# Attention, mixture of experts and feed-forward on one core: stores issued late, ten strided units first, single PSUM banks at attention's end, zero matmuls that read data, extra run fifth

## The chip, the cores and the metric

The kernel runs on one NeuronCore of a Trainium2 chip. It is one program with five instruction queues: TensorE (PE, its weight loads shown as PEld), VectorE (DVE), ScalarE (ACT), GpSimd (POOL) and the queue that only starts transfers (SP). Transfers between memory and SBUF are shared by 16 DMA engines. The metric is the device time of the whole program in microseconds (us). One execution with the hardware profiler gives the trace from which all rows come.

## The reference

Causal attention in 4 batches of 576 positions with 8 heads of 64: heads 0 to 3 attend to the last 32 positions ("local"), heads 4 to 7 to earlier positions of the same residue modulo 32 ("strided"). The result, 2304 tokens of 512 features, goes through a mixture of 8 experts of which each token takes one, then through a feed-forward layer with a squared ReLU.

```python
scores = where(mask, q @ k.T / 8, -1e9); x = softmax(scores) @ v      # mask: local or strided
logits = x @ w_gate + modality_bias[modality_id]
e = argmax(logits, 1); gate = softmax(logits)[e]
x[e == i] = gate * (relu(x[e == i] @ w1[i]) @ w2[i])                  # for each expert i
out = relu(x @ w_in) ** 2 @ w_out
```

All is float32. The products of the experts and of the feed-forward layer are made of three products each, on operands split in a rounded part ("hi") and its rest ("lo").

## The kernel before

**Attention.** The work is cut in 40 units: 22 strided ones of up to 108 tokens and 18 local ones of 128 tokens (`units`). A step k of the loop over units issues, for several units at once, the stages of a pipeline: `norm(k-4)` (VectorE divides by the sum of the softmax, into the tile `xn`, and POOL stores `xn` in the table `x1` in memory), the loads of a later group of units (`loads_to`, on SP), `stage_s(k)` (scores, PE), maximum and subtraction (VectorE) and the exponential (ScalarE), `features(k-5)` (transposed copy of `xn` into `xT`, products with the gate's weights), `stage_t(k-2)` (PE transposes the probabilities) and `stage_v(k-3)` (product with v). Seven strided units come first, then strided and local ones in turn, and three local ones last. Loads go in groups of one or two units into `NLD` buffers. Each engine runs its own instructions in the order in which they are written and waits on semaphores for the others; `stage_s` issues `KEEP` matmuls of zeros (`warm`).

**The end of attention** (from `stage_t(L - 1)` on) finishes the last five units with PSUM tiles of two banks ("sp", "xp") and three times six matmuls of zeros (`dense`). Then the gate's logits of the last tiles are made: `products` (gate's weights times `xT`), `fetch` (ScalarE copies them), `folds` (PE sums them), `add` (VectorE adds the bias), `rt.local` (VectorE: maximum, one-hot `oh`).

**Routing** (`Routing.finish`) counts the tokens of each expert (`cp`), finds every token's place in the sorted order (`pos`, `pab`), builds one-hot matrices `ohb` (by VectorE, ScalarE and POOL, 18 slices) and `pay`, and multiplies them in 18 matmuls into `ip`, the sorted list of tokens (`idn`). `keep(n)` issues n matmuls of zeros, 512 columns each.

**Experts** (`moe_and_ffn`). The sorted list is worked off in nine runs of 256 places and one extra run of 128 (for places in which a second expert begins), each of 8 chunks. A chunk loads 512 KB of an expert's weights (SP), splits them (ScalarE hi, VectorE lo), and PE does `mm1` and `mm2`. In between, by a table of chunks (`conv`), 16 halves of the feed-forward layer's weights (512 KB each, `load_half`) are loaded and converted. POOL gathers the tokens of a run by an indirect transfer. A loop (`extra_loop`) for further extra runs is in the program and is not entered with these inputs. **The feed-forward layer** follows, 6 blocks of 384 tokens.

Of the kernel before, what the change touches and what calls it, by code (L numbers as in the profile page):

```python
# [33 lines left out]
N2A = 7  # L34
NCV = 4
HOLD = 5
KEEP_R = (6, 11, 24)
KEEP_D = 6
# [4 lines left out]
S_FIRST = 7  # L43
NWM = 5
NLD = 8
# [28 lines left out]
def attention_and_routing(es, tc, a, x1, res):  # L74
# [8 lines left out]
    ps = es.enter_context(tc.tile_pool(name="a_ps", bufs=2, space=PSUM))  # L83

    def bank(tag):
        if tag == "xp":
            return ps.tile([128, 2, 512], F32, tag=tag, name=tag, bufs=1)[:, 0]
        return ps.tile([128, 512], F32, tag=tag, name=tag, bufs=1)
# [12 lines left out]
    rt.spare = lambda: ps.tile([128, 2, 512], F32, tag="sp", name="dm")  # L101
# [4 lines left out]
    while ns < NST or nl < NTL - 3:  # L106
        if nl < NTL - 3 and (ns == NST or nl * (NST - S_FIRST) <= (ns - S_FIRST) * (NTL - 3)):
# [8 lines left out]
    for kind, sizes in (("s", (1, 1, 1) + (2,) * 9 + (1,)), ("l", (1, 1) + (2,) * 8)):  # L116
        t0 = 0
        for n in sizes:
            groups.append((kind, t0, n))
            t0 += n  # L120
# [147 lines left out]
    def v_norm3(k):  # L268
        kind, t, n, w, gi, o = geom(k)
        xn = wk.tile([128, 256], F32, tag="xn", name="xn", bufs=8)  # L270
# [3 lines left out]
        )  # L274
        if kind == "l":
# [10 lines left out]
        st[k, "x"] = xn  # L286

    def stage_x(k, xq):
# [5 lines left out]
        if kind == "l":  # L294
            ac.activation(out=xT[:, 0:2, 128 * t:128 * t + 128], in_=src, func=AF.Copy)
            return
# [13 lines left out]
        while c < end:  # L310
# [5 lines left out]
            ac.activation(out=tok, in_=src[:, :, a0:a0 + NJ * m].rearrange("p c (m j) -> p c m j", j=NJ), func=AF.Copy)  # L316
# [19 lines left out]
    def fetch(t0, t1, src):  # L336
        lt = wk.tile([128, 256], F32, tag="lt", name="lt", bufs=2)[:, 0:128 * (t1 - t0)]
        ac.activation(out=lt, in_=src[:, 0:128 * (t1 - t0)], func=AF.Copy)
        return t0, t1, lt
# [61 lines left out]
    for k in range(NU):  # L401
        if k >= LN:
            norm(k - LN)
        side(1)
# [26 lines left out]
    def two(tag):  # L431
        return ps.tile([128, 2, 512], F32, tag=tag, name=tag + "t", bufs=1 if tag == "xp" else 2)
# [5 lines left out]
    stage_t(L - 1)  # L438
    norm(L - 3)
    stage_x(L - 4, bank("xq"))  # L440
    sb = two("sp")
    stage_v(L - 2, sb[:, 0])
    sc = two("sp")
    stage_t(L, sc[:, 0])
    if lt_p:
        add(folds(lt_p.pop(0), sc[:, 1]))
    xb = two("xp")
    stage_v(L - 1, xb[:, 0])
    stage_x(L - 3, sb[:, 1])
    stage_v(L, xb[:, 1])  # L450
    norm(L - 2)
    norm(L - 1)
    t0, t1 = lg_done[0], lg_ready(L - 2)
    assert t1 - t0 <= 2 and NTL - t1 == 3
    if t1 > t0:
        lq = bank("xq")
        products(t0, t1, lq)
        lt_p.append(fetch(t0, t1, lq))
    lp = bank("pp")
    products(t1, NTL - 1, lp, (2, 3))  # L460
    norm(L)
    sd = two("sp")
    dense(sd[:, 1], KEEP_D)
    stage_x(L - 2, sd[:, 0])
    if lt_p:
        add(folds(lt_p.pop(0), bank("xq")))
    todo += [rt.local(loc, t1)]
    se = two("sp")
    dense(se[:, 1], KEEP_D)
    stage_x(L - 1, se[:, 0])  # L470
    products(t1, NTL - 1, lp, (0, 1))
    sf = two("sp")
    dense(sf[:, 1], KEEP_D)
    stage_x(L, two("xp")[:, 0])
    lt_p.append(fetch(t1, NTL - 1, lp))
    add(folds(lt_p.pop(0), bank("xq")))
    side(100)
    lr = sf[:, 0]
    products(NTL - 1, NTL, lr)
    add(folds(fetch(NTL - 1, NTL, lr), bank("pp")))  # L480
# [5 lines left out]
class Routing:  # L486
# [95 lines left out]
    def finish(self):  # L582
# [5 lines left out]
        def keep(n):  # L588
            for i in range(n):
                pe.matmul(dm[:, i % 2], lhsT=self.warm[:, 0:128], rhs=self.warm, start=True, stop=True)  # L590

        keep(KEEP_R[0])
        cp = bank("xp")
# [50 lines left out]
        for i in range(n_ac):  # L644
            ac.activation(out=ohb[:, nb + i, :], in_=self.iob, func=AF.Square, scale=-1.0, bias=pab[:, 1, nb + i:nb + i + 1])
        if n_ac:
            ac.activation(out=ohb[:, nb:nb + n_ac], in_=ohb[:, nb:nb + n_ac].bitcast(F32), func=AF.Relu, scale=-1.0, bias=1.0)
# [12 lines left out]
        order = list(range(nb, T)) + list(range(nb))  # L660
# [17 lines left out]
    def extras(self, buf, gs, idf):  # L678
# [6 lines left out]
        def t_(n):  # L685
# [5 lines left out]
                         in1=xv[:, 2, :].unsqueeze(2).to_broadcast(s7t), op=ALU.is_equal)  # L691
        pk = t_(7 * T).rearrange("p (x t) -> p x t", x=7)
        xs = t_(21).rearrange("p (q x) -> p q x", q=3)
        for qi, src in enumerate((idf, es_, gs)):
            ve.tensor_tensor(out=pk, in0=so, in1=src.unsqueeze(1).to_broadcast(s7t), op=ALU.mult)  # L695
            ve.tensor_reduce(out=xs[:, qi], in_=pk, axis=AX.X, op=ALU.add)  # L696
        ve.tensor_copy(res["xidn"], xs[:, 0])
        xm = t_(7)
        ve.tensor_tensor(out=xm, in0=xs[:, 1], in1=xv[:, 1, :], op=ALU.is_equal)
        ve.tensor_tensor(out=xs[:, 2], in0=xs[:, 2], in1=xv[:, 0, :], op=ALU.mult)  # L700
        ve.tensor_tensor(out=res["xgm"], in0=xm, in1=xs[:, 2], op=ALU.mult)

    def side_ops(self, op):
# [37 lines left out]
        def xruns():  # L741
            ve.tensor_tensor(out=w77, in0=self.lt7, in1=flb, op=ALU.mult)
            ve.tensor_reduce(out=rk, in_=w77, axis=AX.X, op=ALU.add)
            ve.tensor_tensor(out=sel, in0=self.k9[:, 0:7].unsqueeze(2).to_broadcast(s77),
                             in1=rk.unsqueeze(1).to_broadcast(s77), op=ALU.is_equal)
            ve.tensor_tensor(out=sel, in0=sel, in1=flb, op=ALU.mult)
            o7 = off[:, 1:8]
            ve.tensor_tensor(out=tmp1, in0=o7.unsqueeze(1).to_broadcast(s77), in1=o7.unsqueeze(2).to_broadcast(s77),
                             op=ALU.is_lt)
            ve.tensor_reduce(out=bx[:, 0], in_=tmp1, axis=AX.X, op=ALU.add)  # L750
            ve.tensor_single_scalar(out=bx[:, 1], in_=offf[:, 1, 1:8], scalar=128.0, op=ALU.is_le)
            ve.tensor_tensor(out=bx[:, 0], in0=bx[:, 0], in1=self.e17, op=ALU.subtract)
# [557 lines left out]
```

## Time and profile before

| | us |
|---|---|
| median of 3 runs (lowest, highest) | 771.91 (768.98, 772.53) |
| the profiled execution's own time | 772.12 |
| its span, first to last instruction | 770.3 |
| PE busy (share of the span) | 749.7 (97%) |
| VectorE, ScalarE, POOL busy | 422.1, 345.9, 92.6 |

The profiled execution lies 0.2 us above the median, and its own time 1.8 us above its span: the span is what the rows divide. "Busy" of PE counts matmuls whose ends are modelled, so a stretch of 100% isn't one at full speed. A row of a timeline gives the start and the length in us, and in brackets the engine's idle time ahead of it with what ended it. PEclk is the granted clock of TensorE as a share of 2.4 GHz (0.50 is 1.2 GHz).

### The profile page before, as it was taken

To read this page: it belongs to the slowest core of one execution; us is meant where nothing else is said; L and a number is where in the kernel's file an instruction comes from. 1 tells how busy PE (TensorE), PEld (TensorE's weight loads), DVE (VectorE), ACT (ScalarE), POOL (GpSimd) and SP (SyncE) were. 2 spreads that over 40 slices of the span, in tenths; PEclk is the share of its full clock that TensorE was granted. 3 is DMA by queue.
4 is the path that set the end of the run, shared out by engine and by line. 5 is a ranking of instruction groups with operands and counts; after the bars stand their busy time and mean duration, and the time that the engine had idled before them with its cause. 6 is when DMAs were issued, how large, how long until landed. Compare 5 with 4: busy or idle time off the path is not lost.

```text
span 770.3 us, 14540 instructions
## 1 busy us (share of the span) xinstructions
PE 749.7 (97%) x5785; PEld 672.5 (87%) x5787; DVE 422.1 (55%) x845; ACT 345.9 (45%) x678; POOL 92.6 (12%) x118
## 2 busy tenths in 40 slices
PE   9899979999999999999999999999999999999996
PEld 5676746999899999999898998989899899989995
DVE  5776856788878788874896322332332232233221
ACT  3554634566766666654776322322332232233221
POOL 8543422101100010000000100010010001001001
PEclk9999998999999999999999999999999999999999
DMA  8999206678776877763361100000010000001001
GB/s 216 277 275 262 81 24 224 197 256 264 249 255 222 272 236 233 236 206 123 119 185 53 41 1 1 14 27 1 1 43 0 1 14 28 0 1 42 1 0 42
DMA packets 31709, 90.97 MB, mean 118 GB/s; under 512 B 8050, under 2 KB 9282, under 8 KB 31638
## 3 DMA queue, kind: packets, MB, share of 16 engines
q1 hardware_dynamic: 23446, 75.27, 31.5%
q0 software_dynamic: 8192, 14.74, 5.8%
q8 instruction: 46, 0.75, 0.4%
q14 instruction: 25, 0.20, 0.1%
HBM read 80.52 MB, written 9.44 MB: 117 GB/s over the span
## 4 chain that ended last, share of the span: by engine, by line
PE 78%; DVE 2%; DMA 1%; ACT 1%; issue 1%; POOLq 0%; DVEq 0%
PE fhp L1040 26%; PE op L1065 26%; PE hp L829 13%; PE yp L840 13%; DVE w L799 1%; PE tp L818 1%; DMA stg<-in_wcat_dram 1%; ACT w L795 0%; DMA out_dram<-ob,idn 0%; DVE xl L822 0%; POOLq L1306 0%; DVE hl L834 0%; ACT xh L821 0%; DVE xt L695 0%; DVE xt L696 0%
## 5 line engine op out<-in xcount | busy, mean ns | idle before, releaser
L1040 PE MATMUL fhp<-xh,w 128*128 128x384 f32 x768 | 211.1, 337 | 0.0
L1052 DVE TENSOR_TENSOR r<-fhp,r 128x384 f32<-128x384 f32 x80 | 44.6, 558 | 223.0 <-ACT gh L1050 211.9
L1043 ACT ACTIVATE r<-fhp 128x384 f32<-128x384 f32 x96 | 47.1, 491 | 244.2 <-PE fhp L1040 244.2
L1040 PEld LDWEIGHTS fhp<-xh,w 128*128 128x128 f32 x768 | 140.6, 188 | 4.0
L1065 PE MATMUL op<-w,gh 128*128 128x512 f32 x546 | 141.9, 395 | 0.0
L1040 PE MATMUL fhp<-xl,w 128*128 128x384 f32 x384 | 130.1, 339 | 0.0
L1065 PEld LDWEIGHTS op<-w,gh 128*128 128x128 f32 x546 | 101.3, 188 | 16.9
L799 DVE TENSOR_TENSOR w<-stg,w 128x1024 fp32r<-128x1024 f32 x80 | 97.6, 1220 | 20.6 <-ACT w L795 19.4
L829 PE MATMUL hp<-xh,w 128*128 128x256 f32 (+1 forms) x640 | 101.4, 281 | 2.7 <-ACT w L795 1.5
L829 PEld LDWEIGHTS hp<-xh,w 128*128 128x128 f32 x640 | 87.3, 189 | 4.6 <-ACT w L795 1.9
L795 ACT ACTIVATE w<-stg 128x1024 fp32r<-128x1024 f32 x80 | 84.1, 1053 | 12.0 <-DVE mk L738 6.1
L840 PE MATMUL yp<-hh,w 128*128 128x256 f32 x576 | 81.0, 283 | 0.0
L1065 PE MATMUL op<-w,gl 128*128 128x512 f32 x273 | 78.2, 394 | 0.0
L1040 PEld LDWEIGHTS fhp<-xl,w 128*128 128x128 f32 x384 | 72.1, 188 | 3.9
L840 PEld LDWEIGHTS yp<-hh,w 128*128 128x128 f32 x576 | 73.3, 189 | 0.0
L1075 POOL DMA_INDIRECT out_dram<-ob,idn x18 | 18.8, 1043 | 441.7 <-ACT ob L1073 412.0
L1055 DVE TENSOR_TENSOR gl<-r,gh 128x384 fp32r<-128x384 f32 x91 | 50.8, 558 | 21.9 <-ACT r L1054 14.4
L832 ACT ACTIVATE hh<-hp 128x256 fp32r<-128x256 f32 (+1 forms) x80 | 29.8, 372 | 72.0 <-PE hp L829 70.9
L1065 PEld LDWEIGHTS op<-w,gl 128*128 128x128 f32 x273 | 51.4, 188 | 12.1
L829 PE MATMUL hp<-xl,w 128*128 128x256 f32 (+1 forms) x320 | 50.9, 281 | 0.0
L1050 ACT ACTIVATE gh<-r 128x384 fp32r<-128x384 f32 x91 | 47.8, 526 | 2.9
L840 PE MATMUL yp<-hl,w 128*128 128x256 f32 x288 | 45.8, 280 | 0.0
(219 smaller groups left out, 842.6 us busy)
## 6 DMA issues: line engine op xcount, KB each, us to landing
stg<-in_wcat_dram SPq DMA_DIRECT2D x80, 512.0 KB
stg<-in_w2cat_dram SPq DMA_DIRECT2D x32, 512.0 KB
qk<-in_qkl_dram SPq DMA_DIRECT2D x8, 576.0 KB
qk<-in_qks_dram SPq DMA_DIRECT2D x9, 432.0 KB
v<-in_vl_dram SPq DMA_DIRECT2D x8, 396.0 KB
x<-xn POOLq DMA_DIRECT2D x18, 128.0 KB, 6.9
x<-xn POOLq DMA_DIRECT2D x40, 54.0 KB, 7.8
v<-in_vs_dram SPq DMA_DIRECT2D x18, 111.4 KB
```

The costliest lines, as they stand in the source:

```text
L795: ac.activation(out=w[:, 0, :], in_=t, func=AF.Copy)
L799: ve.tensor_tensor(out=w[:, 1, :], in0=t, in1=w[:, 0, :].bitcast(F32), op=ALU.subtract)
L829: pe.matmul(hp, lhsT=w[:, wi, 128 * k:128 * k + 128], rhs=x[:, k, 0:n], start=(i == 0), stop=(i == 11))
L832: ac.activation(out=hh, in_=hp, func=AF.Relu)
L840: pe.matmul(yp[c // 2][:, SLOT * (c % 2):SLOT * (c % 2) + SLOT], lhsT=w[:, wi, 512 + 128 * c:640 + 128 * c], rhs=x, start=(j == 0 and x is ...
L1040: pe.matmul(hp, lhsT=w[:, wi, 128 * k:128 * k + 128], rhs=x[k], start=(i == 0), stop=(i == 11))
L1043: ac.activation(out=r, in_=hp, func=AF.Relu)
L1050: ac.activation(out=gh, in_=r, func=AF.Square)
L1052: ve.tensor_tensor(out=r, in0=hp, in1=r, op=ALU.mult)
L1055: ve.tensor_tensor(out=gl, in0=r, in1=gh.bitcast(F32), op=ALU.subtract)
L1065: pe.matmul(op[t], lhsT=x[:, 128 * t:128 * t + 128], rhs=w[:, wi, 512:1024], start=(j == 0 and first), stop=(j == NC2 - 1 and last))
L1075: gp.indirect_dma_start(out=out[:, :], out_offset=bass.IndirectOffsetOnAxis(ap=idn[:, i:i + 1], axis=0), in_=ob, in_offset=None,)
```

## The change

- A unit's store in `x1` is no longer written in `norm`, but taken from a list (`stores`) at the start of a later step, up to 16 units behind; `xn` has 20 buffers (8 before), loads have 7 (8 before).
- Ten strided units first (7 before), seven local ones last (3 before).
- At the end of attention a new pool of eight single banks takes the place of the two-bank tiles; the order of the stages is new, 2 matmuls of zeros stand where 18 stood, and the last tile's logits are made without the copy and the sum.
- In routing, six matmuls of zero weights read `oha` and `pay` as soon as these are written; `ohb` of ScalarE comes in two pieces, and the 18 matmuls take another order. `keep` has 7, 9 and 12 matmuls (6, 11 and 24).
- At the start of the experts the first loads and splits have a new order, nine matmuls read the first split weights (`busy`), and both gathered blocks are scaled by ScalarE.
- The extra run is the fifth of ten (third before). Its small VectorE work (29 instructions) goes out two at a time, one pair a chunk. The 16 halves are spread over 62 chunk positions which leave out ten around the extra run.

```diff
-KEEP_R = (6, 11, 24)          -KEEP_D = 6     -S_FIRST = 7      -NLD = 8
+KEEP_R = (7, 9, 12)           +KEEP_D = 2     +S_FIRST = 10     +NLD = 7
+XR = 4                        +DEFER = 16     +L_LAST = 7
...
     def v_norm3(k):
-        xn = wk.tile([128, 256], F32, tag="xn", name="xn", bufs=8)
+        xn = wk.tile([128, 256], F32, tag="xn", name="xn", bufs=DEFER + 4)
...
+        stores.append((k, xn))
...
+    def store():
+        k, xn = stores.pop(0)
         kind, t = geom(k)[0:2]
         if kind == "l":
             gp.dma_start(out=x1[t * 128:t * 128 + 128, 0:256], in_=xn)
...
         if k >= LN:
             norm(k - LN)
+        while len(stores) > max(1, min(DEFER, DEFER + 20 - k)):
+            store()
...
+    pse.close()
+    pd.append(es.enter_context(tc.tile_pool(name="a_pd", bufs=1, space=PSUM, reuse_waits="tile")))
+    for tag in ("xp", "xr", "a0", "a1", "b0", "b1", "pp", "xq"):
+        bank(tag)
+    stage_t(L - 1, bank("a0"))
+    stage_x(L - 4, bank("xq"), True)
+    stage_v(L - 2, bank("a1"))
...
+        gated(oha.rearrange("p t a -> p (t a)").bitcast(BF16)[:, 0:512])
...
+            if v == 0:
+                gated(pay[:, 0:14, 0, :].bitcast(BF16))
...
-        order = list(range(nb, T)) + list(range(nb))
+        order = [*range(nb, nb + 4), *range(6), *range(nb + 4, T), *range(6, nb)]
...
-    rl.insert(2, run_x(0))
+    rl.insert(XR, run_x(0))
...
+    free = [m for m in range(4, n_ch - 4) if not NC1 * XR - 4 <= m < NC1 * XR + 6]
     for i in range(2 * N2A + 2):
-        conv.setdefault(9 * i // 2 + 5, []).append(lambda j=j, hf=hf: load_half(j, hf, stg_p))
+        p = free[len(free) * i // (2 * N2A + 2)]
+        conv.setdefault(p, []).append(lambda j=j, hf=hf: load_half(j, hf, stg_p))
...
-            if m == 2:
-                res["xruns"]()
-            if m == 3:
-                res["extras"](tmp_p.tile([128, 512], F32, tag="cv", name="xt", bufs=NCV))
+            if m >= 2:
+                for _ in range(2):
+                    next(xops, None)
```

What POOL has ahead of the first stores, in the kernel before (the number behind a name is the buffer, and the semaphores for which a row waits stand in brackets):

```order
L509 DMA cbc_264<-in_cb_dram 128x450
L511 DMA iob_266<-in_io_dram 128x128
L284 DMA x1_60<-xn_271 3x18x256 [waits DVE_49]
L284 DMA x1_60<-xn_271 3x18x256
L284 DMA x1_60<-xn_312 3x18x256 [waits DVE_49]
```

And POOL at the same place in the changed kernel:

```order
L534 DMA cbc_261<-in_cb_dram 128x450
L536 DMA iob_263<-in_io_dram 128x128
L558 CAST mf_491<-mid_255 128x18 [waits DMASW0_49]
L559 ISA
L559 TENSOR_SCALAR mi_492<-mf_491 128x18 [waits Pool_49]
L561 TENSOR_TENSOR mb_495<-mf_491,bb_257 128x144 [waits DMASW1_49]
L563 TENSOR_TENSOR mb2_496<-mi_492,bb_257 128x144 [waits Pool_49]
L565 TENSOR_TENSOR mb_495<-mb_495,mb2_496 128x144 [waits Pool_49]
L305 DMA x1_60<-xn_268 3x18x256 [waits DVE_49]
L305 DMA x1_60<-xn_268 3x18x256
L305 DMA x1_60<-xn_312 3x18x256 [waits DVE_49]
```

The five small instructions for the bias (`mf` to `mb`) moved ahead of the stores; the stores themselves still follow each other on POOL with nothing else between, and the semaphore of the first is still the one VectorE raises with that unit's own `xn`.

PE at the end of attention before (`xp`, `spt`, `xpt`, `pp`, `xq` are PSUM tiles; `xn` is transposed by X, `sm` by T, `v` multiplied by V):

```order
L240 MATMUL xp<-v,pt 64x65 x4
L223 MATMUL pp<-ident,sm 96x128 x4
L292 MATMUL xq<-ident,xn 128x128 x2
L251 MATMUL spt<-v,pt 64x65 x8
L223 MATMUL spt<-ident,sm 96x128 x4
L251 MATMUL xpt<-v,pt 64x65 x8
L292 MATMUL spt<-ident,xn 128x64 x2
L251 MATMUL xpt<-v,pt 64x65 x8
L333 MATMUL xq<-xT,wg 32x256 x4
L333 MATMUL pp<-xT,wg 32x256 x2
L436 LDWEIGHTS warm
L436 MATMUL spt<-warm 128x256
```

PE at the end of attention in the changed kernel (`a_`, `b_` are the new single banks):

```order
L230 MATMUL a_2000<-ident,sm 96x128 x4
L312 MATMUL xq<-ident,xn 128x128 x2
L258 MATMUL a_2011<-v,pt 64x65 x8
L230 MATMUL pp<-ident,sm 96x128 x4
L258 MATMUL b_2032<-v,pt 64x65 x8
L312 MATMUL b_2046<-ident,xn 128x128 x2
L258 MATMUL xp<-v,pt 64x65 x8
L312 MATMUL a_2064<-ident,xn 128x128 x2
L312 MATMUL xq<-ident,xn 128x128 x2
L364 MATMUL xr<-fold,lt 128x8
L353 MATMUL a_2075<-xT,wg 32x256 x4
L353 MATMUL pp<-xT,wg 32x384 x2
```

The transposes of the last `xn` tiles now stand ahead of the products with the gate's weights and have no matmuls of zeros between them; each has a bank of its own.

PE in routing in the changed kernel, between the second `keep` and the 18 matmuls into `xp`, where before the last matmul of `keep` and the 18 stood next to each other:

```order
L615 LDWEIGHTS warm
L615 MATMUL a_2127<-warm 128x512
L620 LDWEIGHTS warm
L620 MATMUL a_2127<-oha,warm 128x512
L620 LDWEIGHTS warm
L620 MATMUL a_2128<-oha,warm 128x512
L620 LDWEIGHTS warm
L620 MATMUL a_2127<-oha,warm 128x512
L620 LDWEIGHTS warm
L620 MATMUL a_2127<-pay,warm 128x504
...
L695 MATMUL xp<-pay,ohb 128x54 x18
```

Six matmuls that wait for VectorE's `oha` and `pay` were put ahead of the 18.

## Rows read from the trace of the kernel before

**Rows 1.** Busy time by stage: loop, end of attention, routing, experts, feed-forward.
```profile
core 0: us, PE busy (x) PEld busy (x) DVE busy (x) ACT busy (x) POOL busy (x), PEclk, DMA share, GB/s
0.00:92.74 92.74, 86.57 (x1630) 62.19 (x1630) 65.63 (x210) 48.09 (x148) 47.85 (x73) 0.98 0.84 228
92.74:109.06 16.32, 13.80 (x154) 9.36 (x155) 7.29 (x32) 6.16 (x17) 2.95 (x5) 0.90 0.13 43
109.06:127.74 18.68, 15.19 (x68) 8.11 (x67) 12.24 (x46) 7.86 (x14) 4.88 (x6) 0.81 0.49 166
127.74:357.06 229.32, 227.36 (x1897) 225.35 (x1898) 185.91 (x289) 143.62 (x226) 18.14 (x17) 1.00 0.72 236
357.06:770.30 413.24, 406.73 (x2040) 367.54 (x2039) 151.02 (x270) 140.21 (x274) 18.77 (x18) 1.00 0.09 29
```

**Rows 2.** Timeline of POOL, stores of three successive strided units.
```profile
57.78 1.22 POOL L284 DMA_DIRECT2D x<-xn  x2 [1.74 <-DVE xn L271]
62.20 1.23 POOL L284 DMA_DIRECT2D x<-xn  x2 [1.74 <-DVE xn L271]
69.40 1.23 POOL L284 DMA_DIRECT2D x<-xn  x2 [4.54 <-DVE xn L271]
```

**Rows 3.** Timeline of PE, its long waits in the loop over units.
```profile
22.32 0.56 PE L193 MATMUL sp<-qk 64*64 64x96 f32 x16 [0.80 <-DMA qk<-in_qkl_dram]
29.80 0.42 PE L193 MATMUL sp<-qk 64*54 64x54 f32 x16 [1.11 <-DMA qk<-in_qks_dram]
64.58 0.24 PE L181 MATMUL sp<-mloc,identb 128*128 128x192 bf16 x1 [1.30 <-issue]
```

**Rows 4.** Busy time and granted clock in short stretches (columns as in Rows 1).
```profile
104.00:106.00 2.00, 0.97 (x12) 0.68 (x12) 0.81 (x5) 0.74 (x4) 0.00 (x0) 0.99 0.00 0
106.00:108.00 2.00, 1.67 (x5) 1.01 (x7) 1.55 (x9) 0.27 (x2) 0.00 (x0) 0.50 0.00 0
118.00:120.00 2.00, 2.00 (x6) 0.76 (x5) 1.76 (x15) 0.00 (x0) 1.08 (x1) 0.50 0.99 389
```

**Rows 5.** DMA queues from 12 to 24 us: packets, MB, share of the engines.
```profile
q1 hardware_dynamic: 1089, 2.59, 82.6%
q0 software_dynamic: 778, 0.58, 20.0%
```

**Rows 6.** Timeline of the end of attention, PE and VectorE.
```profile
97.70 0.55 PEld L251 LDWEIGHTS xpt<-v,pt 96*64 96x64 f32 x16
98.14 0.16 DVE L261 TENSOR_SCALAR rs<-spt 128x4 f32<-128x4 f32 x1 [2.80 <-ACT xT L316]
100.03 0.42 DVE L271 TENSOR_TENSOR xn<-xpt,rs 128x256 f32<-128x256 f32 x1
103.30 0.38 PE L292 MATMUL xpt<-ident,xn 128*128 128x128 f32 x2
107.80 0.26 DVE L579 TENSOR_TENSOR oh<-eq,m 128x24 bf16<-128x24 f32 x1
109.06 0.21 PE L594 MATMUL xp<-cbc,oh 128*128 128x2 bf16 x1
```

**Rows 7.** Timeline of routing: one-hot slices and the 18 matmuls.
```profile
113.18 0.58 DVE L655 TENSOR_TENSOR pay<-oha,glo 128x324 fp32r<-128x324 f32 x1
114.47 1.35 DVE L640 TENSOR_TENSOR ohb<-iob,pab 128x384 fp32r<-128x384 f32 x3
114.91 2.92 PE L662 MATMUL xp<-pay,ohb 128*128 128x54 f32 x18 [2.03 <-ACT ohb L647]
```

**Rows 8.** Timeline from the second gather to the first expert matmul.
```profile
125.07 0.49 DVE L1009 TENSOR_SCALAR xg<-xg,gmask 128x512 f32<-128x512 f32 x1 [0.68 <-DMA xg<-x,idn]
127.74 1.22 PE L829 MATMUL hp<-xh,w 128*128 128x256 f32 x8 [0.74 <-ACT xh L821]
```

**Rows 9.** Timeline of PE in the experts, its two waits of note.
```profile
147.44 0.74 PE L829 MATMUL hp<-xh,w 128*128 128x256 f32 x4 [0.45 <-DVE w L799]
195.15 0.74 PE L829 MATMUL hp<-xh,w 128*128 128x256 f32 x4 [1.46 <-ACT w L795]
```

More of the change, by code (lines that the diff above doesn't have):

```diff
@@ L100, in attention_and_routing @@
     rt.warm = warm
-    rt.spare = lambda: ps.tile([128, 2, 512], F32, tag="sp", name="dm")
+    rt.spare = lambda: (bank("a0"), bank("a1"))
     units = []
@@ L115, in attention_and_routing @@
     groups, gof = [], {}
-    for kind, sizes in (("s", (1, 1, 1) + (2,) * 9 + (1,)), ("l", (1, 1) + (2,) * 8)):
+    for kind, sizes in (("s", (1, 1, 1, 1) + (2,) * 9), ("l", (2,) * 9)):
         t0 = 0
@@ L274, in v_norm3, with move @@
         )
+        stores.append((k, xn))
+        st[k, "x"] = xn
+    def move(on_ve, out, in_):
+        if on_ve:
+            ve.tensor_copy(out, in_)
+        else:
+            ac.activation(out=out, in_=in_, func=AF.Copy)
+    stores = []
+    def store():
+        k, xn = stores.pop(0)
+        kind, t = geom(k)[0:2]
         if kind == "l":
@@ L429, in attention_and_routing, with logit @@
     L = NU - 1
-    def two(tag):
-        return ps.tile([128, 2, 512], F32, tag=tag, name=tag + "t", bufs=1 if tag == "xp" else 2)
+    def logit(tgt, t, t0, cs, first=False):
+        for c in cs:
+            pe.matmul(tgt[:, NE * (t - t0):NE * (t - t0) + NE], lhsT=xT[:, c, 128 * t:128 * t + 128],
+                      rhs=wg[:, c, 0:NE], start=(first and c == cs[0]), stop=(c == 1), skip_group_check=True)
     def dense(tgt, n):
@@ L471, in attention_and_routing @@
+    assert lg_ready(L - 3) == t1 and t1 - t0 == 2
+    lp = bank("a1")
+    products(t0, t1, lp)
+    lt_p.append(fetch(t0, t1, lp))
+    lp, lr = bank("pp"), bank("b0")
+    products(t1, NTL - 1, lp, (2, 3))
+    stage_x(L, bank("b1"))
     products(t1, NTL - 1, lp, (0, 1))
-    sf = two("sp")
-    dense(sf[:, 1], KEEP_D)
-    stage_x(L, two("xp")[:, 0])
+    lf = bank("a0")
+    folds(lt_p.pop(0), lf)
     lt_p.append(fetch(t1, NTL - 1, lp))
-    add(folds(lt_p.pop(0), bank("xq")))
+    logit(lr, NTL - 1, NTL - 1, (2, 3), True)
@@ L477, in attention_and_routing @@
+    logit(lr, NTL - 1, NTL - 1, (0, 1))
+    add((t0, t1, lf[:, 0:NE * (t1 - t0)]))
+    for _ in rt.local(loc, t1):
+        pass
+    lf = bank("xq")
+    dense(lf, KEEP_D)
+    add(folds(lt_p.pop(0), lf))
+    add((NTL - 1, NTL, lr[:, 0:NE]))
+    while stores:
+        store()
     side(100)
-    lr = sf[:, 0]
-    products(NTL - 1, NTL, lr)
-    add(folds(fetch(NTL - 1, NTL, lr), bank("pp")))
     for _ in rt.local(t1, NTL):
@@ L643, in finish @@
         nb = T - n_gp - n_ac
[L644 to L647, printed above, removed]
+        na = nb + n_ac
+        for i0, i1 in ((nb, nb + 4), (nb + 4, na)):
+            for i in range(i0, i1):
+                ac.activation(out=ohb[:, i, :], in_=self.iob, func=AF.Square, scale=-1.0, bias=pab[:, 1, i:i + 1])
+            ac.activation(out=ohb[:, i0:i1], in_=ohb[:, i0:i1].bitcast(F32), func=AF.Relu, scale=-1.0, bias=1.0)
         for i in range(T - n_gp, T):
@@ L995, in prep, with busy @@
             transp(xgs.pop((r, h)), h, *xt[r])
+    def busy(w, v):
+        tp = ps.tile([128, 512], F32, tag="tp", bufs=2, name="busy")
+        for i in range(3):
+            pe.matmul(tp, lhsT=w[:, v, 0:128], rhs=w[:, v, 0:512], start=True, stop=True)
     for h in range(2):
         g(0, h)
-    for n in range(3):
+    for n in range(2):
         issue_load(n)
     n_x = nc.values_load(regs[0:1, 23:24], min_val=1, max_val=7)
-    for n in range(SP):
-        wt[n] = split_hi(staged[n], wM)
-        if n < 2:
-            split_lo(staged.pop(n), wt[n])
+    issue_load(2)
+    issue_split(0)
+    busy(wt[0], 0)
+    busy(wt[0], 1)
+    wt[1] = split_hi(staged[1], wM)
+    busy(wt[1], 0)
     extra_loop()
-    scl(0, 0)
-    ve.tensor_scalar(out=xgs[0, 1], in0=xgs[0, 1], scalar1=rl[0]["gm"][:, 1:2], scalar2=None, op0=ALU.mult)
+    for h in range(2):
+        scl(0, h)
     for h in range(2):
         prep(0, h)
-    split_lo(staged.pop(2), wt[2])
+    split_lo(staged.pop(1), wt[1])
+    issue_split(2)
     for n in range(SP):
```

115 lines of the change are left out of this document (68 added, 47 removed).

## The prediction

> **What bounds the kernel now.** I first cut the span by stage and read each stage's PE and clock [rows 1]. In the last stage, 413.24 us, PE runs without a wait of note and the change leaves its work alone: it is carried over whole. So is PE's work in the experts (227.36 busy of 229.32 us). What a change of order can win lies in the other stages: the loop over units (92.74 us, PE busy 86.57), the end of attention (16.32, of which 13.80) and routing up to the first expert matmul (18.68, of which 15.19, clock 0.81, and much of that is matmuls of zeros). There the time is a chain through all engines, not PE's work, and I read which wait ends last.
>
> **The loop, 92.74 us.** A strided and a local unit together take 4.42 us from one POOL store to the next [rows 2]: 57.78 to 62.20. Three waits of PE stick out [rows 3]: 0.80 and 1.11 us for q and k from memory, and 1.30 us at 64.58 between two matmuls of one tile, for nothing that the profile shows. After the last one the clock fell, and the step took 69.40 - 62.20 = 7.20 us [rows 2], 2.8 us more than the steady one.
>
> The change wants to take the stores out of the way of the loads: from 12 to 24 us the loads take 82.6% and the stores 20.0% of the engines [rows 5]. I don't think that it does. A store stands later in the text, but POOL has nothing else to do between its stores, and what a store waits for is still VectorE's signal for its own `xn` (the fences on POOL above). In the trace each store's idle time ends with just that, `DVE xn` [rows 2]. So POOL will issue it as soon as `xn` is there, as before; only the five bias instructions now come first, and they hold POOL for about a microsecond or two around 13 us.
> The Trainium skill, "DMA: Bandwidth & Descriptors", section "Anatomy of one DMA", speaks the same way against this part: a DMA engine does not wait on semaphores, the issuing sequencer does so before it dispatches. By that rule the stores' times are set by POOL's waits alone; were they held back after all, the sum below would be 2 us lower.
>
> The order of units: each kind keeps its matmuls, so PE's work in the loop stays. Ten strided units first put 3830 KB of loads ahead of the first local scores and their partner, by the tile sizes in the code, where 2560 KB stood; at 2.59 MB in 12 us [rows 5], 216 KB/us, that is 6.0 us later, while three more strided units make it due some 3 x 1.9 = 5.7 us later (1.9 is an estimate, less than half of the 4.42 of a pair, since a strided unit is the smaller). So there is no flood of slack: I expect about 1 us of load waits to remain of 1.91, and credit 0.7. The wait of 1.30 us with its slow clock, 2.8 us, has no cause that the change touches and may or may not come back: half of it, 1.4. Seven load buffers in place of eight still let SP run six groups (about 12 units, some 25 us) ahead. **Loop: -2.1; bounds 0 (both stay) and -4.7 (both go).**
>
> **The end of attention, 16.32 us.** Before, the last unit's product with v begins at 97.70, but its normalisation follows late: VectorE sits idle 2.80 us until 98.14 because a copy by ScalarE holds the two-bank tile, and the last `xn` starts at 100.03. Its transpose then waits on PE behind products and zeros until 103.30. The one-hot is done at 107.80 + 0.26 = 108.06, and the first count, which stands behind six zero matmuls at 1.2 GHz, starts at 109.06 [rows 4, 6].
> After, every stage has its own bank, the last transpose stands ahead of the last products, and 16 of 18 zero matmuls are gone. The last `xn` can follow its product at once: 97.70 + 0.55 + some 0.9 for three VectorE instructions (0.16 and 0.42 are two of them) gives about 99.2 for its end in place of 100.45, and the transpose, now behind one pair of products only, some 100.0 in place of 103.30: -3.3. From there VectorE is the chain: it must do the one-hot of tiles 9 to 13 (five instructions of 0.26 or less) before the adds for the last four and their five, against which the last tile saves its copy and sum (before, 103.30 to 108.06 is 4.76; I take 4.3): -0.4. The first count no longer waits for zeros if the clock holds, up to -1.0. Together -4.7; by what such hand-laid chains lose I take **-4.0; bounds -5 and -1.5**. The five stores at the end cost nothing: POOL has no work until the one-hots of routing.
>
> **Routing, 18.68 us.** The 18 matmuls start at 114.91, 2.03 us late, for ScalarE's whole block of seven slices, and end at 117.83 [rows 7]. After, the first four slices come as a piece of their own, so they can start when `pay` is done, 113.18 + 0.58 = 113.76. The end is set by VectorE's last slices, 114.47 + 1.35 = 115.82, plus the matmuls behind (18 took 2.92, 0.16 each; six or seven remain): about 116.9, -0.9. The six reading matmuls end before 113.8 and hide in PE's idle 2.03. From there the second gather rules: it ends an idle 0.68 us of VectorE at 125.07 [rows 8]; 0.9 earlier it lets the first expert matmul come from 127.74 to about 126.8. The scaling by ScalarE has no row; I take it as 0.2 longer than VectorE's 0.49, against which 12 fewer zeros (six filled 2.00 us [rows 4]) stand ahead of the transposes that follow: 0.4. The nine `busy` matmuls end before the gather lands; without that cover they would cost 2.7 (eight matmuls of half their width took 1.22 [rows 8]: 9 x 2 x 0.15). VectorE's split of the second chunk now comes behind the transposes: its product is only needed a chunk later. **Routing: -1.1; bounds -2.5 and +1.5.**
>
> **Experts, 229.32 us.** PE waited 0.45 us at 147.44 for a split that stood behind the 29 small instructions of the extra run, and 1.46 us at 195.15 for weights late in the extra run, where a chunk is short and halves of the other layer's weights shared the engines [rows 9]. Two small instructions a chunk (29 in 15 chunks, done before the gather of the fifth run needs them) fit in VectorE's free fifth (185.91 busy of 229.32) [rows 1]. No half is loaded within the extra run. The halves stand every 62/16 = 3.9 chunks instead of 4.5: VectorE's load rises by some 2%. **-1.7 of 1.91; bounds -2.3 and +1.**
>
> **Sum.** 772.1 - 2.1 - 4.0 - 1.1 - 1.7 = 763.2. The profiled execution (772.12) stands 0.2 above the median of 771.91, so the sum may be read against either. About 0.5% (3.9 us) is what a measurement of this kernel can tell from no change.
>
> **Rivals.**
> *A. The clock falls in the new gaps.* The clock fell to 1.2 GHz after PE was busy only 0.97 of 2 us at 104 to 106, and stayed there at 118 to 120 although zeros filled PE [rows 4]. The change takes away 16 + 12 zero matmuls, so it may fall earlier at the end of attention, and again while PE waits for the first split weights, with half speed in the first expert chunks. For it: fewer matmuls in the same waits. Against it: the waits get shorter, and the reading and `busy` matmuls stand in the gaps. Price: 1.5 to 2 us at the end (half of some 3 to 4 us of PE work), 1.5 us for the first 12-matmul chunks: 766 to 767.
> *B. Slower: the denser halves starve the experts.* Each half takes SP, ScalarE and VectorE between two chunks. If at 3.9 chunks' distance one can't be worked off before the next, PE waits at each of 16 as it did once, 1.46 us [rows 9]. It decides the sign from 9/16 = 0.56 us a half on; at the full price, 16 x 1.46 = 23 us, 786; at 0.9, 777. Against it: outside the extra run no half made PE wait at 4.5, and 19% of VectorE's time in the stage is free.
> *C. The stores do go later,* or the unexplained wait doesn't return: loads run ahead, the loop gives its -4.7 in place of -2.1: 760.6.
> *D. Nothing to gain at the end:* another engine, ScalarE with its copies or VectorE with the one-hots, takes PE's place, the end gives -1.5, loop and routing 0: 768.9, and up to 770 if the experts keep a wait.
>
> **Chances.** The forecast (761 to 765.5) 0.50; A 0.24; C 0.13; D 0.09; B 0.04. The prediction is the forecast's 763.2. The range 757.5 to 769 leaves out B, the far ends of C and D. Faster by over 0.5% (below 768.0) are the forecast, A, C and a part of D that is small: 0.87; within 0.5% the rest of D: 0.09; slower 0.04.
>
> **What the changed profile would show.** Stores on POOL that start at 13 to 15 us and end their idle time with their own `xn`: my reading of the order; none before 40 us: rival C's. The last scores at about 90 to 91 us, the first count 12 to 13 us behind them, 18 index matmuls that start beside the end of `pay`, the first expert matmul some 17.5 us behind the count, and 227 to 228 us from there to the feed-forward layer, with no wait over 0.5 us in the extra run. A clock of 0.50 at the end of attention or in the first expert chunk would be A; PE waits for `w` that recur every four chunks B. The prediction is wrong if the loop keeps 92 us and the end 15, or if the feed-forward layer, which should keep 413.2 us, moves.

## The result, and the profile after

The changed kernel took 764.48 us (median of 11 runs, 761.98 to 768.92), the kernel before 772.53 beside it (11 runs, 768.98 to 775.74): ratio 0.9901, interval [0.9878, 0.9923]. On the 771.91 of the first runs that is 764.3, against 763.2 predicted. The profiled execution of the changed kernel was a long one (768.88, span 767.1), so one pair of traces tells little of the loop. The stages, cut at the start of the last scores, of the first count, of the first expert matmul and of the first feed-forward matmul (columns as in [rows 1]):

```profile
0.00:94.92 94.92, 86.71 (x1600) 62.39 (x1600) 65.30 (x208) 48.13 (x147) 47.66 (x73) 0.96 0.82 223
94.92:107.71 12.79, 12.69 (x157) 8.72 (x158) 7.81 (x33) 5.75 (x15) 2.71 (x5) 1.00 0.16 56
107.71:125.11 17.40, 14.94 (x68) 8.11 (x69) 11.01 (x46) 7.97 (x16) 5.18 (x6) 0.90 0.38 123
125.11:353.65 228.54, 226.92 (x1896) 225.10 (x1897) 186.39 (x289) 143.72 (x227) 16.59 (x17) 1.00 0.75 241
353.65:767.10 413.45, 406.89 (x2042) 367.70 (x2040) 151.03 (x270) 140.17 (x274) 18.93 (x18) 1.00 0.08 29
```

Against the profiled execution of before: loop +2.2, end -3.5, routing -1.3, experts -0.6 (229.16 before by the cut used here, 356.90 - 127.74), last stage unchanged; -3.2 in all, where the medians say -8. Most of the difference lies in the loop, which varies from one execution to the next (table below). Its waits, and the clock behind the second stop (timeline of PE, then short stretches):

```profile
16.99 0.42 PE L200 MATMUL sp<-qk 64*54 64x54 f32 x16 [1.46 <-DMA qk<-in_qks_dram]
34.45 0.56 PE L200 MATMUL sp<-qk 64*64 64x96 f32 x16 [0.56 <-DMA qk<-in_qkl_dram]
37.20 0.37 PE L186 MATMUL sp<-warm 128*128 128x256 bf16 x1 [1.00 <-issue]
70.79 0.35 PE L200 MATMUL sp<-qk 64*54 64x54 f32 x9
72.98 0.32 PE L200 MATMUL sp<-qk 64*54 64x54 f32 x7 [1.84 <-issue]
```

```profile
72.00:74.00 2.00, 1.02 (x13) 0.83 (x13) 0.35 (x2) 0.08 (x1) 0.96 (x2) 1.00 1.09 243
74.00:76.00 2.00, 2.00 (x39) 1.46 (x42) 1.37 (x7) 1.00 (x3) 0.10 (x1) 0.70 0.99 260
76.00:78.00 2.00, 2.00 (x18) 1.23 (x18) 1.09 (x2) 0.64 (x3) 0.48 (x1) 0.50 0.71 222
78.00:80.00 2.00, 2.00 (x39) 1.61 (x41) 1.31 (x6) 1.31 (x4) 0.32 (x1) 0.95 0.33 87
```

PE stops in the middle of 16 matmuls of one line, for nothing that the profile shows; then the clock goes to 0.50 for some 3 us, with 18 matmuls in 2 us where 39 stood just before and just after. The trace of before had one such stop [rows 3], this one two.

POOL's stores, with the normalisation that one of them waits for:

```profile
16.00 0.44 POOL L561 TENSOR_TENSOR mb<-mf,bb 128x144 f32<-128x144 f32 x1 [2.17 <-DMA bb<-in_modality_bias_dram]
17.34 4.91 POOL L305 DMA_DIRECT2D x<-xn  x8
71.01 0.42 DVE L278 TENSOR_TENSOR xn<-xp,rs 128x256 f32<-128x256 f32 x1
71.73 1.24 POOL L305 DMA_DIRECT2D x<-xn  x2 [1.75 <-DVE xn L278]
```

They are not held back by 16 units: once POOL has caught up, each follows its own `xn` by 0.3 us (71.73 against 71.01 + 0.42). Only the first four units' stores are late, at 17.34, because the bias instructions now ahead of them wait for `bb` until 16.00.

The end of attention and routing, on PE, VectorE and ScalarE:

```profile
101.29 0.42 DVE L278 TENSOR_TENSOR xn<-xp,rs 128x256 f32<-128x256 f32 x1
102.69 0.44 PE L312 MATMUL b<-ident,xn 128*128 128x128 f32 x2
105.19 0.38 PE L461 MATMUL xq<-warm 128*128 128x256 bf16 x2
107.36 0.29 DVE L604 TENSOR_TENSOR oh<-eq,m 128x32 bf16<-128x32 f32 x1
107.71 0.18 PE L623 MATMUL xp<-cbc,oh 128*128 128x2 bf16 x1
113.70 1.88 PE L695 MATMUL xp<-pay,ohb 128*128 128x54 f32 x14 [0.57 <-DVE ohb L669]
122.99 0.72 ACT L871 ACTIVATE xg<-xg,gmask 128x512 f32<-128x512 f32 x1 [1.40 <-DMA xg<-x,idn]
125.11 1.22 PE L887 MATMUL hp<-xh,w 128*128 128x256 f32 x8 [0.69 <-ACT xh L879]
237.03 0.74 PE L887 MATMUL hp<-xh,w 128*128 128x256 f32 x4 [1.38 <-ACT w L853]
```

From the start of the last scores the last transpose now takes 102.69 - 94.92 = 7.8 us (10.6 before, from [rows 1, 6]), the count follows the one-hot by less than 0.1 us, and the clock holds at the end of attention (1.00). In routing it does not: its mean is 0.90 there. The last row is the wait behind the extra run: it is still there, although no half is loaded in that run.

### The profile page after: what moved, and what is told of

Read it like the earlier page. It is cut to its first block, busy times and chain, and to the rows that moved or that the text cites. A ratio compares the mean times of both kernels' runs of the same rounds, so it can differ in the third digit from the quotient of the medians.

```text
span 767.1 us, 14490 instructions
## 1 busy us (share of the span) xinstructions
PE 748.2 (98%) x5760; PEld 672.0 (88%) x5762; DVE 421.5 (55%) x844; ACT 345.7 (45%) x677; POOL 91.1 (12%) x118
## 4 chain that ended last, share of the span: by engine, by line
PE 90%; DMA 6%; DVE 2%; issue 1%; ACT 1%; SPq 0%; POOLq 0%; DVEq 0%; ACTq 0%
PE fhp L1108 26%; PE op L1133 26%; PE hp L887 14%; PE yp L898 13%; DMA qk<-in_qkl_dram 3%; PE sp L200 2%; PE pp L230 1%; PE xp L258 1%; PE xq L312 1%; DMA qk<-in_qks_dram 1%; PE tp L876 1%; DMA stg<-in_wcat_dram 1%; PE sp L188 1%; DMA xg<-x,idn 1%; PE xp L247 1%
## 5 line engine op out<-in xcount | busy, mean ns | idle before, releaser
L1143 POOL DMA_INDIRECT out_dram<-ob,idn x18 | 18.9, 1052 | 441.5 <-ACT ob L1141 413.5
```

The source lines that it names most:

```text
L1143: gp.indirect_dma_start(out=out[:, :], out_offset=bass.IndirectOffsetOnAxis(ap=idn[:, i:i + 1], axis=0), in_=ob, in_offset=None,)
```

## Experiments

All traces are cut in the same way; that of late_gather is left out, as said there. "Load waits" are PE's waits for `qk` in the loop, "stops" its waits there without a shown cause, in us.

| trace | loop | end | routing | experts | load waits | stops |
|---|---|---|---|---|---|---|
| before | 92.74 | 16.32 | 18.68 | 229.16 | 2.9 | 1.3 |
| before_again | 94.59 | 15.17 | 18.38 | 231.54 | 3.0 | 2.4 |
| changed | 94.92 | 12.79 | 17.40 | 228.54 | 3.4 | 2.8 |
| again | 90.98 | 12.79 | 18.81 | 227.16 | 3.8 | 0.7 |
| store_now | 93.73 | 12.79 | 17.61 | 227.03 | 3.8 | 1.1 |
| first7 | 96.55 | 12.79 | 18.19 | 227.05 | 3.7 | 3.0 |
| held | 94.36 | 12.79 | 17.27 | 230.74 | 2.2 | 2.5 |
| more_zeros | 91.22 | 12.78 | 18.85 | 226.86 | 1.5 | 1.7 |
| old_halves | 93.09 | 12.79 | 18.42 | 229.32 | 2.9 | 2.1 |
| no_zeros | 93.84 | 12.66 | 20.02 | 227.88 | 2.1 | 3.1 |
| old_end_parts | 91.91 | 14.54 | 17.75 | 227.93 | 1.9 | 4.1 |
| few_v | 89.92 | 12.79 | 17.22 | 226.82 | 0.7 | 2.3 |
| before_few_v | 87.38 | 15.17 | 18.63 | 228.35 | 0.5 | 1.0 |

The last stage lies between 413.40 and 413.50 in all of them.

**again and before_again: the two kernels once more.**

> The changed kernel without an edit, for a second trace. The prediction's theory (the stops of PE for which the profile shows no wait, each followed by about 3.4 us of half clock, come and go between executions and cost some 3 us each): the end of attention 12.8 us, routing 17.4 and the experts 228.5 stay within 0.3, the loop up to the last scores' start is 88 to 89 us without a stop, 91 to 92 with one, 95 with two. Rival (the new order of units itself makes the loop 2 us longer): two stops at the same places and 94.9 us again.

> The kernel before, for a second trace. Theory (the loop gained nothing lasting, the stops come and go): loop up to the last scores' start 89 to 93 us with load waits of 2 to 4 us, end 16.3, routing 18.2 to 19, experts 228.5 to 229.2 with the wait of some 1.5 us behind the extra run. Rival (that wait and that loop are fixed properties of the order): stop of 1.3 us at 64.6 and wait of 1.46 us at 195 again.

Changed again: 766.02 us (median of 12), ratio 0.9924 [0.9894, 0.9955]; before again one execution, 774.91. The stops sat elsewhere each time (76.99 of 0.69 us; 52.18 and 60.16 of 1.36 and 1.08), so they are no property of the order; the rival falls. The end came as expected in again, but routing (18.81 for 17.4) and the experts (227.16 for 228.5) did not stay within 0.3, and in before_again the loop, the end and the experts all missed. The loop with one stop was 90.98, and the clock kept 1.00 behind that short stop, but fell behind a load wait of 1.71 us at 27.06. The wait behind the extra run was absent in again; before_again had 0.78 us there for weights and 0.71 us for a split of VectorE, and a clock of 0.50 to 0.72 from 126 to 134 us, around the first expert chunks, which lengthens its experts. Before's end was 15.17, with a mean clock of 0.98 instead of 0.90.

**store_now: no list.**

```diff
         stores.append((k, xn))
+        store()
```

> Each store is issued in the normalisation again, as in the kernel before; the rest is the changed kernel. The prediction's theory (the list holds no store back, POOL waits for its own xn in both): the time within 1 us of the changed kernel, the first stores at 12.5 to 14 us instead of 17.3 because only the five bias instructions move back behind the first stores. Rival (later stores make room for the loads): first load waits of PE longer than the 3.4 us in sum of the changed kernel, the time 2 to 3 us longer.

768.23 us, ratio 0.9953 [0.9923, 0.9983]; first stores at 11.47 us (12.5 to 14 expected), the load waits 3.8 as in again. The median is 2.2 us above again's, against the 1 us that the theory allowed, but the intervals overlap, and the traced loop lies among those of the changed kernel. Neither a gain of the list nor its absence is shown.

**held: stores that are really late.**

```diff
         k, xn = stores.pop(0)
+        if stores:
+            gp.tensor_copy(hold1, stores[-1][1][0:64, 0:1])
```

> The changed kernel with a copy of 64 numbers on POOL ahead of each store, which reads the newest normalised unit in the list; so each store is really held back, by up to 16 units. Theory of the prediction's rival C (stores that go later leave the engines to the loads): no store before 40 us, load waits of PE from 3.4 to 4.3 us down to under 2 us, the loop to the last scores' start 1.5 to 2.5 us shorter (90 to 92 us with one stop), the time 1.5 to 2.5 us under the changed kernel's. Rival (the same bytes meet the later loads instead): load waits move or stay, stops stay, the time within 1 us.

770.10 us, ratio 0.9976 [0.9954, 0.9999], some 4 us slower than again by the ratios, whose intervals just touch. Timeline of POOL and PE:

```profile
44.60 1.33 POOL L309 DMA_DIRECT2D x<-xn  x2
237.09 0.74 PE L891 MATMUL hp<-xh,w 128*128 128x256 f32 x4 [2.11 <-ACT w L857]
```

No store before 44.60, load waits down to 2.2 (under 2 expected): that much was nearly right. But the transfers stay full (share 1.00 at 48 to 60 us), the loop is not shorter (94.36), and a wait of 2.1 us of PE for VectorE's `lg` appears in it: VectorE itself had stood 2.3 us, until a late store landed, before it could write the next `xn`. So late stores, the declared aim of that part, did not pay with 20 buffers for `xn`; the median speaks for a loss. The wait of 2.11 us in the experts is no sign of that, since the changed kernel has had one too (1.38). Rival C of the prediction falls, and it is as well that the list holds nothing back.

**first7: the old head of the order.**

```diff
-S_FIRST = 10
+S_FIRST = 7
```

> Seven strided units first instead of ten, the rest as in the changed kernel. The prediction's theory (ten first relieve the loads by some 0.7 us): PE's load waits grow by 0.5 to 1 us, the time 0.5 to 1 us longer. Rival (ten strided units in a row want their 3.8 MB sooner than the engines bring it, which the waits of 0.86, 1.46 and 0.53 us say): the load waits fall by 0.5 to 1.5 us and the time by as much.

768.07 us, ratio 0.9955 [0.9929, 0.9981]. Load waits 3.7 us, neither more nor fewer: both expectations miss. The longer traced loop goes with three stops (3.0 us) and a clock of 0.50 behind the last. The median speaks for ten first, without proof.

**few_v and before_few_v: fewer loads.**

```diff
+        if kind in v_kind:
+            v_t[gi] = v_kind[kind]
+            return
+        n = 2
```

> The tile v is loaded for the first two units of each kind alone and used by all units, so some 5 MB of loads are left out (the result is not the reference's). Theory 1 (the stops of PE without a shown wait come from transfers that are full): the transfers' share falls under 0.85, load waits and stops go, the loop to the last scores' start is 86 to 88 us, the time 2 to 5 us shorter than the changed kernel's. Rival (the stops have nothing to do with the loads): the load waits go, stops of 1 to 2 us with half clock remain, and the loop stays at 90 us or more.

> The kernel before with the tile v loaded for two units of each kind alone and used by all, the same omission as in the changed kernel's run with few loads of v (the result is not the reference's); that run had 761.7 us and times within 1.8 us of each other. Theory (the change gains at the end of attention, in routing and in the experts, some 6 to 7 us, and next to nothing in the loop): 768 to 769 us, the ratio of the two 0.991 to 0.992, and the loop to the last scores' start within 1 us of that run's 89.9. Rival (the loop's new order is worth 2 us or more without the crowd of loads too): 770 us or more and a loop 2 us longer.

761.68 us (five runs, 760.66 to 762.43) and 765.66 us (eight runs, 764.75 to 768.74): ratio of the medians 0.9948, -4.0 us, so the expected 768 to 769 was missed, and the rival's 770 too. The loops, few_v first (columns as in [rows 1]):

```profile
0.00:89.92 89.92, 85.68 (x1601) 61.86 (x1601) 65.25 (x208) 48.09 (x147) 47.62 (x73) 0.96 0.58 174
```

```profile
0.00:87.38 87.38, 84.73 (x1630) 61.48 (x1630) 65.48 (x210) 48.02 (x148) 47.89 (x73) 1.00 0.59 179
```

The 2.5 us between them go with few_v's stop of 1.94 us at 23.84 (0.98 in the other) and a clock of 0.50 behind it, from 24 to 30 us; no gain of the order shows here. Of few_v's two expectations neither holds whole: the time is 4.3 us under again's, as theory 1 said, but a stop remains and the loop is 89.92 for 86 to 88. Both kernels keep their early stop, at 23 to 24 us, where the transfers are still full (share 1.02 in few_v); behind 40 us, where the share is 0.43 and 0.38, there is none in either. Leaving the loads out brings the kernel before 0.8% (ratio 0.992) and the changed one 0.5% (0.9873 against again's 0.9924). So some 2 us of the change's gain may exist only where loads crowd. That is not shown: the intervals are nearly as wide, and few_v's longer stop would by itself narrow the gap.

**old_halves and late_gather: the wait behind the extra run.**

```diff
-        p = free[len(free) * i // (2 * N2A + 2)]
+        p = 9 * i // 2 + 5
```

```diff
+            d = 2 if m // NC1 == XR + 1 else 0
+            if d and m % NC1 == 0:
+                g(m // NC1 + 1, 0)
+                g(m // NC1 + 1, 1)
-                g(r + 2, 0)
+            if j == 3 + d and r != XR:
+                g(r + 2, 0)
```

> The changed kernel with the old table for the halves of the feed-forward layer's weights (every 4.5 chunks, two or three of them in the extra run). Theory 1 (the halves in the extra run make its weights late): a wait of 1 to 1.5 us of PE behind the extra run in each trace, experts 228.5, the time 1.4 us longer than the changed kernel. Theory 2 (the gathers of tokens, 0.26 MB each, which fall into the short chunks, and how the transfers happen to lie, make them late): a wait or none as in the changed kernel's traces, the time the same within 0.5 us.

> The changed kernel with the two gathers of tokens that fall into the extra run moved into the first chunk of the next run (scaling and transposes of that run two chunks later). Theory 2 of old_halves (gathers in the short chunks make weights late): no wait over 0.3 us behind the extra run, experts 227.0, the time up to 1 us shorter than the changed kernel. Rival (the extra run asks for 512 KB every 2.45 us whatever else moves): a wait as in the changed kernel, no gain.

old_halves: 767.74 us, ratio 0.992 [0.9888, 0.9952], no longer than the changed kernel (again's ratio is 0.9924); that is theory 2's time, but intervals of some 5 us can't exclude theory 1's 1.4. late_gather: 769.34 us, 0.9947 [0.991, 0.9983], not better than the changed kernel; its traced execution took 781.48, 12 us above its median, and isn't read here. The experts in old_halves, by stretch and on PE's timeline:

```profile
124.30:353.62 229.32, 228.18 (x1897) 225.39 (x1897) 186.71 (x290) 143.06 (x227) 17.38 (x17) 1.00 0.73 240
```

```profile
235.07 0.67 PE L887 MATMUL hp<-xh,w 128*128 128x128 f32 x4 [0.56 <-DVE w L857]
```

229.32 against 226.82 to 228.54 in the eight traces with the new table (held, with 230.74, and late_gather apart): one trace, but it lies with the three of before (228.35 to 231.54). The wait of PE in it is only 0.56 us, though, under theory 1's 1 to 1.5. In the nine traces with the new table the wait is over 1 us in two (1.38 and 2.11), 0.30 in one, absent in six; before had 0.8 to 1.5 us in three of three. So it is rarer in the changed kernel. That the table does this is not shown, since no difference shows in the time with the old table; and the table does not remove the wait, since weights can come late in the extra run without any half. What makes them late then, the gathers or the pace of one chunk in 2.45 us, stays open.

**no_zeros: no idle matmuls from the end of attention on.**

```diff
-KEEP_R = (7, 9, 12)           -KEEP_D = 2
+KEEP_R = (0, 0, 0)            +KEEP_D = 0
-    busy(wt[0], 0)
...
-        gated(oha.rearrange("p t a -> p (t a)").bitcast(BF16)[:, 0:512])
```

> The changed kernel without the matmuls that compute nothing in its end of attention, routing and start of the experts: no zeros, no reading matmuls, none of the nine on the first split weights. The clock's theory (rival A of the prediction): without them the clock is 0.50 for several us in routing and in the first chunks of the experts, routing 1 to 3 us longer, the first expert chunks up to 1.5 us. Rival (these stretches are a chain of the other engines, PE's clock matters little): within 0.7 us of the changed kernel, routing even 0.3 shorter.

769.98 us, ratio 0.9963 [0.9927, 0.9999], against again's 0.9924. Routing by stretch, and PE's timeline in it:

```profile
106.50:126.52 20.02, 7.74 (x33) 6.11 (x33) 10.99 (x46) 7.88 (x16) 5.44 (x6) 0.50 0.42 124
```

```profile
111.31 4.36 PE L692 MATMUL xp<-pay,ohb 128*128 128x54 f32 x18 [3.37 <-DVE off L756]
121.74 1.11 PE L873 MATMUL tp<-ident,xg 128*128 128x128 f32 x4 [6.07 <-ACT xg L868]
```

The 18 matmuls take 4.36 us at 0.50 (1.2 GHz; 2.19 at full clock in old_end_parts, below): routing 20.02, 2.0 above the mean of 17.97 of the eight traces that keep the new routing. At the end of attention the two zeros do nothing (12.66, clock 0.99). So without zeros, reading and `busy` matmuls the clock is 0.50 through all of routing and until 130.0 us, 3.5 us into the experts, and that costs some 2 us in this trace. What it does not show is which of them matter, nor that they hold the clock all the way. In again, first7 and more_zeros, which have them all, it fell within the index matmuls, which then ended 8.3 to 8.5 us behind the count instead of 7.9; in the changed kernel's first trace it fell just behind them. From again (stretch, then PE):

```profile
111.00:112.00 1.00, 1.00 (x7) 1.00 (x7) 0.00 (x0) 0.00 (x0) 0.00 (x0) 0.50 0.78 115
```

```profile
109.75 2.33 PE L695 MATMUL xp<-pay,ohb 128*128 128x54 f32 x14 [0.57 <-DVE ohb L669]
```

**old_end_parts: three parts put back, one stage each.**

```diff
-KEEP_R = (7, 9, 12)           -KEEP_D = 2
+KEEP_R = (6, 11, 24)          +KEEP_D = 18
-        for i0, i1 in ((nb, nb + 4), (nb + 4, na)):
+        for i0, i1 in ((nb, na),):
-        order = [*range(nb, nb + 4), *range(6), *range(nb + 4, T), *range(6, nb)]
+        order = list(range(nb, T)) + list(range(nb))
```

> The changed kernel with three parts put back, each read in its own stage of the trace: 18 matmuls of zeros ahead of the last fold at the end of attention (2 now); the one-hot slices of ScalarE in one piece with the 18 index matmuls in the old order, without the reading matmuls; zeros of 6, 11 and 24 in routing. Theory of the prediction: end of attention 12.8 + 0.8 to 1.5 us (16 zeros of 0.11 us, some hidden), the index matmuls end 0.9 us later against the count, the first expert matmul 0.5 to 1 us later (17.4 to 18.8 now). Rival (the chain of the other engines rules both): end 12.8 and routing 17.4 to 18.8 as now.

One execution, 767.35 us. Timeline of PE:

```profile
102.18 2.12 PE L461 MATMUL xq<-warm 128*128 128x256 bf16 x18
106.45 0.18 PE L623 MATMUL xp<-cbc,oh 128*128 128x2 bf16 x1 [0.26 <-DVE rsm L575]
112.27 2.19 PE L692 MATMUL xp<-pay,ohb 128*128 128x54 f32 x18 [2.04 <-ACT ohb L677]
```

The end grows by 1.75 us, from 12.79 to 14.54: all of the 16 zeros' time (2.12 against 0.38 us) is on the path, more than expected. The index matmuls wait 2.04 us for ScalarE as before, yet are done 112.27 + 2.19 - 106.45 = 8.0 us behind the count, against 113.70 + 1.88 - 107.71 = 7.9 in the changed kernel: the new order of slices is worth 0.1 in this one pair, and routing stays at 17.75. The clock was 1.00 through all of routing here, without the reading matmuls but with more zeros.

**more_zeros: fill the load wait.**

```diff
-KEEP0 = {0: 0, 1: 4, 2: 4, 3: 4, 4: 4, 5: 4, 6: 3, 7: 3, 8: 3, 9: 2, 10: 2}
+KEEP0 = {0: 0, 1: 4, 2: 4, 3: 4, 4: 4, 5: 4, 6: 3, 7: 3, 8: 3, 9: 2, 10: 2, 11: 8, 12: 4}
```

> The changed kernel with 8 and 4 matmuls of zeros ahead of the scores of units 11 and 12 (1 and 1 before), where PE waited 0.5 to 1.7 us for q and k and the clock fell to 0.50 for some 3 us in the second trace. If that clock costs what it says (half of 3 to 4 us): no clock of 0.50 between 24 and 34 us and the time 0.5 to 1.5 us shorter. Rival (PE waits for loads there anyway, so its speed is free): the same within 0.5 us, or 0.5 us longer by the zeros.

764.95 us, ratio 0.9921 [0.989, 0.9952], again's 0.9924. The clock stayed full from 24 to 34 us and the load waits were the shortest of all runs with every load (1.5), but the clock fell at 50 to 56 behind a stop of 1.72 us. No gain that can be measured, and so no version that clearly beats the changed kernel.

## Why the prediction was right, point by point

**Stores.** Right: the list changes no store's wait, and steady stores follow their own `xn` by 0.3 us. By the Trainium skill ("DMA: Bandwidth & Descriptors", "Anatomy of one DMA") only the issuing sequencer waits, and this trace agrees; in held, where POOL itself waits, the stores do go late. Wrong in size: "they hold POOL for about a microsecond or two around 13 us". POOL stood until 17.3, because it waited for `bb` until 16.0. What the list is worth in time stays open (store_now).

**The loop, -2.1.** The step that credited 0.7 us to ten strided units first is not borne out. It began from 1.91 us of load waits, where the trace of before has 2.9 (also 0.65 us at 10.05 and 0.27 at 26.60), and load waits were 1.9 to 3.8 us in the five traces with the changed loop (changed, again, old_halves, no_zeros, old_end_parts), 2.9 and 3.0 before. The other step, half a stop, was a guess about something that both kernels have, from 0.7 to 4.1 us in one execution. The five loops have a mean of 92.95, before's two 93.67: -0.7, with a scatter of 4 us. The times with and without loads of v hint at -2. Its size stays open; if -2.1 is about right, that is luck, since one step is not borne out and the other was a guess. The last scores came at 94.92 us in the first trace and at 90.98 in again, where 90 to 91 was expected.

**The end, -4.0.** Right in kind: -3.5 against the profiled execution, 12.8 us in every trace of the table that keeps the new end. The last transpose came 2.8 us earlier (3.3 predicted), the rest gave 0.7 (1.4 predicted). The shares were seen wrongly, though. Before's end at a nearly full clock is 15.17, and with 18 zeros put back in one place it is 14.54: of the 2.4 us that last, some 1.75 are then zeros that stood in the chain, and some 0.6 what banks and order bring. That is an estimate: before's 18 stood in three places, and no run has the old banks without them. The other 1.1 of the 3.5 goes with the half clock of one execution [rows 4].

**Routing, -1.1.** -1.3 in the first pair, -0.6 over the means (17.97 of eight, 18.56 of before's three). In the first pair the index matmuls ended 0.9 us sooner, as predicted (7.9 us behind the count, 8.8 before by [rows 6, 7]), but the cause was mis-sized: by old_end_parts the pieces are worth 0.1, and the rest goes with before's clock, 0.50 from about 116 us on. From there the second gather rules, as predicted; its length, and in three traces the clock, move routing between 17.2 and 18.9.

**Experts, -1.7.** Right in kind: the mean of the eight traces is 227.4, of before's three 229.7, -2.3; without before_again, whose first chunks ran slow, it is -1.3. The wait of 0.45 us for a split behind the small instructions is in all three traces of before and gone in every trace of the changed kernel. "No half is loaded within the extra run" does not end the other wait: it came back in the traced execution with 1.38 us, over the 0.5 that the prediction allowed.

**Sum and rivals.** -0.7 - 2.8 - 0.6 - 2.3 = -6.4 by means of traces (before's end 15.55 over three), against -7.6 and -5.9 by the two measured ratios and -8.9 predicted. Three terms of four were too large by 0.5 to 1.4 us, so the kinds of gain were foreseen but a median within 1.1 us of the forecast was luck in part. Of the two signs of being wrong, the loop did keep 92 us in the mean (92.95), the end did not keep 15. B never showed: no waits for `w` every four chunks. D falls with an end of 12.8. A did not come where it was placed: with the change the clock held at the end of attention and in the first expert chunks. It came in routing, in part, as it had before. There the prediction misread [rows 4]: before's clock did not "stay" at 1.2 GHz from 106 to 120 us, it was full again from 110 to 116 and fell a second time, after PE had been busy 0.89 and 1.09 of 2 us:

```profile
110.00:112.00 2.00, 2.00 (x11) 1.02 (x12) 1.79 (x11) 0.27 (x1) 0.20 (x1) 1.00 0.00 0
112.00:114.00 2.00, 0.89 (x5) 0.20 (x2) 1.93 (x6) 1.97 (x8) 2.00 (x3) 1.00 0.00 0
114.00:116.00 2.00, 1.09 (x10) 1.09 (x10) 1.76 (x6) 0.86 (x1) 0.23 (x1) 1.00 0.00 0
116.00:118.00 2.00, 2.00 (x11) 1.80 (x11) 0.13 (x2) 0.00 (x0) 0.00 (x0) 0.55 0.64 166
```

## What to carry to other kernels

Before a stage's gain is read from two traces, trace one kernel twice: here the same loop took 91 or 95 us, and the first pair showed -3.2 us where the medians showed -8. A store "issued later" in the text isn't later if its queue has nothing else to do and its wait stays the same; whether lateness would help can be tested by making it real. Matmuls of zeros paid here where PE waits for another engine (2 us in routing, with the reading and `busy` matmuls) and cost their full length where PE is itself the chain (1.75 us at the end); each figure is from one trace.

## What was not expected of the hardware

PE's stops go with packets of an instruction queue, q8. In each trace q8 moves one packet of 16 KB every 4 to 10 us in the loop, and for 25 of the 27 stops in the table's traces the last packet before a stop's end begins 2.4 to 3.1 us ahead of it (held's two: 4.1 and 1.4). In the stretch from 70 to 71 us of the changed kernel, before the stop that ended at 72.98 (packets, MB, share), there is this one, and none from 71 to 73:

```profile
q8 instruction: 1, 0.02, 7.8%
```

The kernel before has one from 61 to 62 us, ahead of its stop to 64.58. That points to instructions that come late. That full transfers make them late (share 1.09 from 72 to 74 us) is not shown: no run moves these packets alone, the packets ahead of stops took 1.0 to 1.6 us and the others 0.9 to 1.8, and few_v had a stop of 0.37 us at 38.31 with the share at 0.54 from 36 to 39 us. The Trainium skill ("Runtime: NRT & Kernel Launch", "Instruction fetch mechanics") says that a sequencer refills its instructions in blocks of 256 over a DMA queue of its own and that the cost of a block's boundary is mostly hidden; if the stops are such boundaries, it was not hidden at each of them here.

A stop can cost nearly as much again through the clock: 1.84 us of stop were followed by 4 us at 0.70 and 0.50, by estimate 0.3 x 2 + 0.5 x 2 = 1.6 us of PE's work. Yet old_end_parts had six stops of 0.3 to 0.9 us, 4.1 in all, and kept a clock of 1.00 and a loop of 91.91.
